# Another written-out order for a fused attention and token/channel mixer kernel: new seeds of the planner and a new order of loads

## The chip, the cores and the metric

The kernel runs on one core of one Trainium2 chip. The metric is the time of one execution on the device, in microseconds (us); lower is better. The core has five engines that run side by side and wait for each other through semaphores: TensorE (PE, matmuls; PEld is its loading of weights), VectorE (DVE), ScalarE (ACT), GpSimd (POOL), which here issues most loads, and SyncE (SP), which here issues transposing DMAs and stores. Each engine works through its own instructions strictly in the order in which they were written.

## The reference

Attention with 8 heads over 576 positions, 8 batches, a causal window of 128 and a linear bias per head, then an MLP mixer, first over the tokens and then over the channels:

```python
scores = scale * np.matmul(q, k.transpose(0, 1, 3, 2))        # q, k, v: (8, 8, 576, 64)
mask = (rel >= 0) & (rel < 128)                               # rel = pos[:, None] - pos[None, :]
scores = np.where(mask, scores + bias[None], -1e9)            # bias = -slope[h] * |rel|
attn = softmax(scores)                                        # over the last axis
x = (attn @ v), heads side by side                            # (8, 576, 512)

h = np.maximum(x.transpose(0, 2, 1) @ w_tok1, 0.0) @ w_tok2   # w_tok1 (576, 256), w_tok2 (256, 576)
u = x + h.transpose(0, 2, 1)
out = u + np.maximum(u @ w_ch1, 0.0) @ w_ch2                  # w_ch1 (512, 1536), w_ch2 (1536, 512)
```

Inputs and output are float32; the kernel computes in bfloat16 with float32 sums.

## The kernel before, in words

**Tiles.** The 576 positions of a batch are four blocks of 128 and a rest of 64. Batches go in pairs: blocks 0 to 3 belong to the first batch of a pair, 4 to 7 to the second, and block 8, the tail, holds both rests.

**Stages.** `side(b)` makes what the channel mixer of batch `b` needs. For each block the q and k tiles (`qk`) are turned (`qkT`; on PE at L681 with a copy at L687 for the first blocks, by a DMA that SP issues at L670 for the later ones), the scores are made on PE (L724), exponentiated on ACT (L759, L746), masked on DVE (L769, L751), multiplied with `v` on PE (L804) and divided by the sum of the row into `xb` (L817 and L820 on DVE, or L826 on ACT). `token_mix(b)` follows: W1 times `xb` (L849, and L859 for the tail), a relu (L867 on ACT or L868 on DVE) into `r10` or `r11`, W2 times that (L891, L887 for the tail), and the sum with `xb` into `ub` or `utl` (L909 on DVE). `ub` is turned into `uT`, on PE (L926) for the first two batches and by a DMA from SP (L917) for the others. `main(b)` is the channel mixer: chunks of WC1 times `uT` (L1087, L1072 for the first pieces of batch 0, L1131 for tails; L1008 where a unit of seven smaller products takes the place of four chunks), their relus (L1093, L1094 and others), sums on DVE (L1112 `s`, `r`), and the second product (L1328, L1220 for tails) as seven products of halves, whose weights include four sums of quarters of WC2, `WT`, made once on DVE at L598. Each product is taken up by DVE at L1291 into a buffer that is stored.

**What sets the order.** No engine's order is written by hand. Every piece of work is entered in a `Plan` with an engine, an expected cost, a rank and the buffers it uses. `Plan.run` goes through time by the plan's own costs, picks for each engine among the ready pieces by time and rank, and gives out buffers and PSUM banks; the pieces are then emitted in the order so found. That order is what the program keeps: on the chip, nothing is picked again. `side(b+1)` and `main(b)` are ranked so that they interleave. A table `SEEDS` shifts the rank of every piece in a group (stage times 10 plus a running part of 30 pieces) by a pseudo-random amount of at most `SHIFT` = 1500; groups that are not in the table are not shifted. Where a piece may run on ACT or on DVE, the plan picks that too.

**Loads.** POOL issues all loads in the order of the string `LOADS` and then block by block for the later pairs. `q2` is the q tile of block 2 of the first pair, `W1` and `W2` the two token weights (W1 brings half of `W1p` with it, `P1` brings the other half), `T0` the part `W2t` of W2 for the tail, `A0` to `A3` the quarters of WC1 and `B0` to `B3` those of WC2. A load is issued only when its buffer is free and when the load eight places earlier has landed.

**Fillers.** Early in the program, where the plan has PE waiting, `emit` puts matmuls on zeros (L1420) into a free PSUM bank. L515 zeroes a part of one `pe` buffer that a later matmul reads.

Of the kernel before, what the change touches and what calls it, by code (L numbers as in the profile page):

```python
# [64 lines left out]
def offset(o):  # L65
    seed = SEEDS.get(o.group, 0)
    z, full = (seed << 20) + o.part * 1000 + o.at, (1 << 64) - 1
    z = (z + 0x9E3779B97F4A7C15) & full
    z = ((z ^ (z >> 30)) * 0xBF58476D1CE4E5B9) & full
    z = ((z ^ (z >> 27)) * 0x94D049BB133111EB) & full  # L70
    return ((z ^ (z >> 31)) >> 11) * 2.0**-52 - 1.0 if seed else 0.0


class Plan:
# [235 lines left out]
    def emit(self, spin):  # L310
# [11 lines left out]
        for _, _, go in sorted(work, key=lambda w: w[:2]):  # L322
# [20 lines left out]
RANKH = 0  # L343
RELU = 350
SUMS_AT = 60e3
SEEDS = {4: 101440, 5: 787032, 6: 757153, 8: 103423, 10: 747690, 11: 468454, 12: 753267, 20: 739044, 21: 923522, 22: 509005, 23: 528472, 30: 196195, 31: 885075, 40: 886354, 41: 184683, 42: 921347, 50: 122991, 51: 204193, 60: 609045, 62: 920468, 70: 169615, 73: 856563, 80: 485548, 81: 308774, 82: 443378, 90: 121380, 91: 900109, 92: 158454, 100: 446306, 101: 820311, 102: 110347, 110: 183021, 111: 737037, 112: 44421, 120: 445134, 121: 47942, 122: 813192, 130: 923735, 131: 191992, 132: 371665, 140: 693539, 141: 260420, 142: 463672, 150: 60451, 151: 574542, 152: 386295, 153: 745919, 154: 632491}
GROUP = 30
SHIFT = 1500.0
UNIT_LATE = False
# [28 lines left out]
EARLY = 1  # L378


LOADS = ("q2 T0 k2 k8 k1 q1 v2 v3 q8 v1 v0 k5 v8 W2 W1 q4 q5 "
         "k4 q7 q6 k6 A2 A0 k7 v7 B0 A3 v4 A1 v5 B1 B2 B3 P1 v6")


@with_exitstack
def kernel(
# [16 lines left out]
    P = nc.NUM_PARTITIONS  # L403
# [6 lines left out]
    R = S - NC * P  # L410
# [18 lines left out]
    plan = Plan()  # L429
# [38 lines left out]
    W1 = const.tile([P, NC, DTOK], BF16, name="W1")  # L468
    W1p = const.tile([P, 2, DTOK], BF16, name="W1p")
    W2 = const.tile([P, NJ, NC * P], BF16, name="W2")  # L470
# [20 lines left out]
    pe_, act_, dve_ = nc.tensor, nc.scalar, nc.vector  # L491
# [19 lines left out]
            act_.activation(out=masks[:, e, i, :, :], in_=dist[:, :, :], func=ACT.Exp, scale=-float(slopes[h]))  # L511
    for t in plan.rings["v"].slots:
        dve_.memset(t[:, :, D : D + 1], 1.0)
    for t in plan.rings["pe"].slots[0:1]:
        dve_.memset(t[:, :, :, :, R:P], 0.0)  # L515

    held = {}
    def turns_of(pr):
# [41 lines left out]
    plan.items = []  # L560
    for item in LOADS.split():
        what, n = item[:-1], int(item[-1])
# [893 lines left out]
```

## Time and profile before

| | us |
|---|---|
| median of 3 runs | 275.4 (275.15 to 275.79) |
| the profiled execution's own time | 275.81 |
| its span, first to last instruction | 273.7 |
| PE busy | 264.7 (97%) |
| DVE busy | 230.1 (84%) |
| ACT busy | 147.6 (54%) |

The span is what the profile shows of the execution; 2.1 us of its time lie outside it. The granted TensorE clock is 1.0 over the whole span. A busy PE is counted up to the modelled end of each matmul, and those overlap: waits of PE are read from the rows that name what ended an idle time, and from the distance between starts. In rows of the timeline the columns are the start and the length in us from the span's start, the engine, the line, the operation, output and inputs, the shape, the count, and in brackets the idle time ahead of it with what ended it. In rows of the chain they are the start, the length and what it was. A `q` behind an engine's name (POOLq, SPq) marks a DMA that it issues; the length there is that of the issue.

### The profile page before, as it was taken

To read this page: it belongs to the slowest core of one execution; us is meant where nothing else is said; L and a number is where in the kernel's file an instruction comes from. 1 tells how busy PE (TensorE), PEld (TensorE's weight loads), DVE (VectorE), ACT (ScalarE), POOL (GpSimd) and SP (SyncE) were. 2 spreads that over 40 slices of the span, in tenths; PEclk is the share of its full clock that TensorE was granted. 3 is DMA by queue.
4 is the path that set the end of the run, shared out by engine and by line. 5 is a ranking of instruction groups with operands and counts; after the bars stand their busy time and mean duration, and the time that the engine had idled before them with its cause. 6 is when DMAs were issued, how large, how long until landed. Compare 5 with 4: busy or idle time off the path is not lost.

```text
span 273.7 us, 7090 instructions
## 1 busy us (share of the span) xinstructions
PE 264.7 (97%) x2803; PEld 188.5 (69%) x2832; DVE 230.1 (84%) x545; ACT 147.6 (54%) x257; POOL 113.2 (41%) x142
## 2 busy tenths in 40 slices
PE   8999999799999999999999999999999999999994
PEld 4665658475568565775778868685678676888883
DVE  7586799988996687966999889997899899957983
ACT  5492883437930694059940098428932496046820
POOL 8999646950680079303970029500920300040000
PEclk9999999999999999999999999999999999999999
DMA  8999999999999999999999959959996700540016
GB/s 156 154 172 171 192 193 179 152 168 211 129 133 148 199 157 141 163 185 193 121 155 125 237 113 113 138 114 210 188 146 98 211 2 0 79 163 14 0 41 192
DMA packets 167553, 38.71 MB, mean 141 GB/s; under 512 B 155872, under 2 KB 166496, under 8 KB 167520
## 3 DMA queue, kind: packets, MB, share of 16 engines
q0 software_dynamic: 113936, 19.51, 92.0%
q1 hardware_dynamic: 51360, 18.10, 34.6%
q10 hardware_dynamic: 2224, 0.66, 1.2%
q8 instruction: 22, 0.36, 0.6%
q14 instruction: 11, 0.09, 0.1%
HBM read 35.85 MB, written 9.44 MB: 165 GB/s over the span
## 4 chain that ended last, share of the span: by engine, by line
PE 88%; DVE 7%; DMA 2%; issue 1%; DVEq 0%; SPq 0%
PE ps L1328 22%; PE ps L1087 18%; PE ps L1008 10%; PE ps L724 6%; PE ps L804 6%; PE ps L849 5%; PE ps L891 4%; PE ps L1131 4%; PE ps L1420 3%; PE ps L1220 3%; DMA uT<-ub 2%; PE ps L681 2%; DVE WT L598 1%; PE ps L859 1%; DVE ub L909 1%
## 5 line engine op out<-in xcount | busy, mean ns | idle before, releaser
L537 POOL DMA_DIRECT2D v<-in_v_dram x40 | 34.2, 862 | 88.8 <-PE ps L804 83.1
L759 ACT ACTIVATE pe<-ps 128x1024 bf16<-128x1024 f32 (+1 forms) x62 | 56.0, 957 | 18.9 <-PE ps L724 18.5
L1087 PE MATMUL ps<-uT,WC 128*128 128x512 bf16 x214 | 55.2, 379 | 1.5 <-DMA uT<-ub 0.4
L1093 ACT ACTIVATE r<-ps 128x512 bf16<-128x512 f32 x53 | 31.1, 603 | 21.3 <-PE ps L1087 21.0
L1328 PEld LDWEIGHTS <-r 128*128 128x128 bf16 x372 | 35.6, 98 | 6.1 <-issue 0.6
L1087 PEld LDWEIGHTS <-WC 128*128 128x128 bf16 x232 | 20.6, 98 | 20.5 <-issue 0.8
L537 POOL DMA_DIRECT2D qk<-in_q_dram x38 | 32.8, 871 | 1.3 <-DMA v<-in_v_dram 1.0
L537 POOL DMA_DIRECT2D qk<-in_k_dram x38 | 32.8, 870 | 0.9 <-DMA WC<-in_moe_w_ch_dram 0.9
L769 DVE TENSOR_TENSOR pe<-pe,mask 128x1024 bf16<-128x1024 bf16 (+1 forms) x50 | 32.6, 661 | 0.5 <-ACT pe L759 0.2
L1328 PEld LDWEIGHTS <-s 128*128 128x128 bf16 x288 | 27.8, 98 | 4.0 <-issue 0.2
L820 DVE TENSOR_TENSOR xb<-ps,rt 128x256 bf16<-128x256 f32 (+1 forms) x68 | 27.5, 417 | 0.8
L804 PEld LDWEIGHTS <-pe 128*128 128x128 bf16 (+1 forms) x560 | 22.2, 98 | 7.0 <-DVE pe L769 1.3
L804 PE MATMUL ps<-v,pe 128*128 128x65 bf16 (+1 forms) x560 | 25.9, 194 | 0.5 <-DVE pe L769 0.5
L1328 PE MATMUL ps<-WC,r 128*128 128x256 bf16 x192 | 25.1, 273 | 0.1
L1328 PE MATMUL ps<-WT,s 128*128 128x256 bf16 x192 | 24.4, 273 | 0.0
L724 PEld LDWEIGHTS <-qkT 64*128 64x128 bf16 x560 | 14.7, 94 | 11.2 <-issue 9.3
L1328 PE MATMUL ps<-WT,r 128*128 128x256 bf16 x180 | 22.1, 273 | 0.0
L909 DVE TENSOR_TENSOR ub<-ps,xb 128x512 bf16<-128x512 f32 x30 | 19.1, 683 | 1.1 <-PE ps L891 0.9
L746 ACT ACTIVATE pe<-ps 128x1024 bf16<-128x1024 f32 x7 | 7.2, 1023 | 23.1 <-PE ps L724 23.1
L724 PE MATMUL ps<-qkT 64*128 64x128 bf16 (+1 forms) x304 | 19.3, 216 | 0.0
L1291 DVE TENSOR_TENSOR raw<-ps,ub 128x512 f32<-128x512 f32 x23 | 15.7, 686 | 3.3 <-PE ps L1328 3.2
L849 PE MATMUL ps<-xb,W 128*128 128x512 bf16 x57 | 15.8, 379 | 0.4
(120 smaller groups left out, 448.7 us busy)
## 6 DMA issues: line engine op xcount, KB each, us to landing
v<-in_v_dram POOLq DMA_DIRECT2D x32, 128.0 KB, 4.9
qk<-in_q_dram POOLq DMA_DIRECT2D x30, 128.0 KB, 5.0
qk<-in_k_dram POOLq DMA_DIRECT2D x30, 128.0 KB, 5.0
WC<-in_moe_w_ch_dram POOLq DMA_DIRECT2D x8, 384.0 KB, 10.4
out_dram<-raw SPq DMA_DIRECT2D x12, 256.0 KB, 2.7
out_dram<-raw SPq DMA_DIRECT2D x16, 128.0 KB, 3.7
out_dram<-raw POOLq DMA_DIRECT2D x6, 256.0 KB, 2.6
out_dram<-ob SPq DMA_DIRECT2D x5, 256.0 KB, 2.6
```

Of the source, the lines that this page charges most:

```text
L537: nc.gpsimd.dma_start(out=to()[p0 : p0 + n, :, :], in_=rows(src, b, s0, n))
L724: pe_.matmul(wide(e)[:, i, 0 if joint else kind, a:z], lhsT=ts[kb]()[e * D : (e + 1) * D, NHP + i, :], rhs=ts[blk]()[e * D : (e + 1) * D, ...
L759: act_.activation(out=pb()[:, e, :, lo:, c0:c1_], in_=wide(e)[:, :, lo:, c0:c1_], func=ACT.Exp, scale=scale)
L769: dve_.tensor_tensor(out=o, in0=o, in1=heads(mk, es), op=ALU.mult)
L804: pe_.matmul(view()[a:z, at, i, :], lhsT=pb()[:, e, i, kind, a:z], rhs=vb()[:, h, 0 : D + 1], start=m == 0, stop=m == len(mms) - 1, skip_g ...
L820: dve_.tensor_tensor(out=x4(), in0=view()[r0:r1_, :, :, 0:D], in1=rt()[r0:r1_, 0:n, :, :].broadcast_to([r1_ - r0, n, 4, D]), op=ALU.mult)
L849: pe_.matmul(t1[j]()[:, :], lhsT=W1[:, c, j * P : (j + 1) * P], rhs=xb()[:, blk, :], start=c == 0, stop=False)
L909: plan.op("DVE", 690, lambda blk=blk, u=u_of(pr, blk)[1], ht=ht, hs=hs: dve_.tensor_tensor(out=u(), in0=ht()[:, hs], in1=xb()[:, blk, :], ...
L1008: pe_.matmul(bk()[:, c * HS : (c + 1) * HS], lhsT=l(c, cb), rhs=r(cb), start=new and c == 0 and cb == 0, stop=cb == 1, skip_group_check=True)
L1087: pe_.matmul(ct()[:, :], lhsT=WC1[:, cb, t * P : (t + 1) * P], rhs=uT()[:, cb, :], start=cb == 0, stop=cb == NCB - 1)
L1093: plan.op("ACT", 600, lambda t=t, ct=ct: act_.activation(out=r2()[:, t, :], in_=ct()[:, :], func=ACT.Relu), rk, part=(r2, t), uses=[ct], o ...
L1328: pe_.matmul(of(bk, c), lhsT=l(t, c), rhs=w(t), start=first, stop=g == 1 and t == HK - 1, skip_group_check=True)
```

## The change

Two tables of the planner are replaced, and one memset goes. `SEEDS` loses some groups, gains others and has other numbers in all of them; `LOADS` names the same 35 loads in another order. The costs, rules and buffers of the planner stay, and so do all operations; which of the two engines takes a piece that either may take is found anew.

```diff
-SEEDS = {4: 101440, 5: 787032, 6: 757153, 8: 103423, 10: 747690, 11: 468454, ...
+SEEDS = {0: 517497, 4: 785877, 5: 700536, 6: 16714, 7: 413526, 8: 685397, ...
...
-LOADS = ("q2 T0 k2 k8 k1 q1 v2 v3 q8 v1 v0 k5 v8 W2 W1 q4 q5 "
-         "k4 q7 q6 k6 A2 A0 k7 v7 B0 A3 v4 A1 v5 B1 B2 B3 P1 v6")
+LOADS = ("k2 k8 q2 k1 q1 v3 v0 v1 v8 q8 v2 q7 W1 q5 q6 k6 k7 "
+         "W2 v7 v6 k5 A1 q4 A0 k4 B0 A2 v4 A3 B3 B2 v5 P1 T0 B1")
...
-    for t in plan.rings["pe"].slots[0:1]:
-        dve_.memset(t[:, :, :, :, R:P], 0.0)
```

Counted over the whole program, PE has 2839 matmuls where it had 2832; the seven more are fillers (51 where there were 44). DVE has one instruction less than before (the memset, L515) and one piece of work goes over from it to ACT. Lines behind L515 stand two lines lower in the changed kernel (L818 there is L820 here).

The first place is the end of the loads on POOL, where the weights of the channel mixer come (WC_122 is WC1, WC_123 is WC2, the rest are tiles and small weights of the token mixer). Before:

```order
L537 DMA v_75<-in_v_dram 128x8x64
L541 DMA WC_123<-in_moe_w_ch_dram 128x3x512
L541 DMA WC_122<-in_moe_w_ch_dram 128x4x384
L537 DMA v_72<-in_v_dram 128x8x64
L541 DMA WC_122<-in_moe_w_ch_dram 128x4x384
L537 DMA v_74<-in_v_dram 128x8x64
L541 DMA WC_123<-in_moe_w_ch_dram 128x3x512 x3
L541 DMA W1p<-in_moe_w_tok_dram 64x256
L537 DMA v_73<-in_v_dram 128x8x64
```

The same place on POOL in the changed kernel:

```order
L539 DMA WC_123<-in_moe_w_ch_dram 128x3x512
L539 DMA WC_122<-in_moe_w_ch_dram 128x4x384
L535 DMA v_76<-in_v_dram 128x8x64
L539 DMA WC_122<-in_moe_w_ch_dram 128x4x384
L539 DMA WC_123<-in_moe_w_ch_dram 128x3x512 x2
L535 DMA v_72<-in_v_dram 128x8x64
L539 DMA W1p<-in_moe_w_tok_dram 64x256
L539 DMA W2t<-in_moe_w_tok_dram 128x2x64
L539 DMA WC_123<-in_moe_w_ch_dram 128x3x512
```

Before, the last of the 35 loads was the v tile of block 6 (v_73); now it is the quarter B1 of WC2, and the v tiles of blocks 6 and 7 stand further up, behind W2.

The second place is DVE in the middle of `main(0)`, where it makes the sums WT and, between them, divides the values of the last blocks of batch 1 into `xb`. Before:

```order
L598 TENSOR_TENSOR WT<-WC_123 128x768
L844 COPY xt_96<-xb_92 64x512
L598 TENSOR_TENSOR WT<-WC_123,WT 128x768 x2
L817 RECIPROCAL rt_88<-ps 128x4
L1112 TENSOR_TENSOR r_103<-r_103 128x3x256
L817 RECIPROCAL rt_89<-ps 128x4
L817 RECIPROCAL rt_91<-ps 128x4
L817 RECIPROCAL rt_90<-ps 128x4
L820 TENSOR_TENSOR xb_92<-ps,rt_89 128x4x64
L820 TENSOR_TENSOR xb_92<-ps,rt_91 128x4x64
L820 TENSOR_TENSOR xb_92<-ps,rt_90 128x4x64
L598 TENSOR_TENSOR WT<-WC_123,WT 128x768
```

DVE at the same place in the changed kernel:

```order
L596 TENSOR_TENSOR WT<-WC_123 128x768
L815 RECIPROCAL rt_89<-ps 128x4
L818 TENSOR_TENSOR xb_92<-ps,rt_88 128x4x64
L818 TENSOR_TENSOR xb_92<-ps,rt_89 128x4x64
L815 RECIPROCAL rt_90<-ps 128x4
L815 RECIPROCAL rt_91<-ps 128x4
L596 TENSOR_TENSOR WT<-WC_123,WT 128x768
L818 TENSOR_TENSOR xb_92<-ps,rt_91 128x4x64
L596 TENSOR_TENSOR WT<-WC_123 128x768 x2
L596 TENSOR_TENSOR WT<-WC_123,WT 128x768
L1110 TENSOR_TENSOR s_113<-r_103,s_113 128x768
L596 TENSOR_TENSOR WT<-WC_123,WT 128x768
```

Three sums WT and the copy `xt` stood ahead of the last three divisions; now these divisions stand ahead of the four sums that need the last quarters of WC2.

The third place is DVE at the end of `token_mix(6)`, where the four sums `ub` are made that SP then turns into the `uT` of `main(6)`. Before:

```order
L1032 TENSOR_TENSOR r_103<-ps,ob_111 128x2x256
L1032 TENSOR_TENSOR r_103<-ps,ob_110 128x2x256
L1034 TENSOR_SCALAR r_103<-r_103 128x2x256 x2
L1032 TENSOR_TENSOR r_103<-ps,raw_107 128x2x256
L1034 TENSOR_SCALAR r_103<-r_103 128x2x256
L909 TENSOR_TENSOR ub_94<-ps,xb_92 128x512 x4
```

DVE at the same place in the changed kernel:

```order
L1030 TENSOR_TENSOR r_103<-ps,raw_107 128x2x256
L1032 TENSOR_SCALAR r_103<-r_103 128x2x256
L866 TENSOR_SCALAR r_98<-ps 128x512
L1030 TENSOR_TENSOR r_103<-ps,ob_110 128x2x256
L1030 TENSOR_TENSOR r_103<-ps,raw_108 128x2x256
L907 TENSOR_TENSOR ub_94<-ps,xb_92 128x512 x4
```

Two of the relus behind the joins (L1034) left DVE's row, and a relu of the token mixer (L866, which is L868 before) came into it; on PE the last product of the second stage of batch 5 (12 matmuls of 256 columns) now stands ahead of the first chunk of `main(6)` and not behind it.

More of the change, by code (lines that the diff above doesn't have):

```diff
@@ L345 @@
 SUMS_AT = 60e3
-SEEDS = {4: 101440, 5: 787032, 6: 757153, 8: 103423, 10: 747690, 11: 468454, 12: 753267, 20: 739044, 21: 923522, 22: 509005, 23: 528472, 30: 196195, 31: 885075, 40: 886354, 41: 184683, 42: 921347, 50: 122991, 51: 204193, 60: 609045, 62: 920468, 70: 169615, 73: 856563, 80: 485548, 81: 308774, 82: 443378, 90: 121380, 91: 900109, 92: 158454, 100: 446306, 101: 820311, 102: 110347, 110: 183021, 111: 737037, 112: 44421, 120: 445134, 121: 47942, 122: 813192, 130: 923735, 131: 191992, 132: 371665, 140: 693539, 141: 260420, 142: 463672, 150: 60451, 151: 574542, 152: 386295, 153: 745919, 154: 632491}
+SEEDS = {0: 517497, 4: 785877, 5: 700536, 6: 16714, 7: 413526, 8: 685397, 10: 382165, 11: 797072, 20: 274424, 21: 252221, 22: 938434, 23: 229954, 30: 618980, 31: 73962, 40: 48116, 41: 463500, 42: 138947, 50: 698411, 60: 77721, 61: 670382, 62: 980070, 70: 272112, 71: 329646, 73: 863296, 80: 860821, 81: 812390, 82: 698755, 90: 642555, 91: 36162, 92: 820492, 100: 378208, 101: 12283, 102: 666882, 110: 374839, 111: 457165, 112: 228977, 122: 958618, 130: 444343, 131: 112543, 132: 417601, 140: 895813, 141: 108506, 142: 904489, 151: 79725, 152: 698131, 153: 848768, 154: 58892}
 GROUP = 30
```

## The prediction

> **What bounds the kernel now.** I read the busy shares first, then the six stretches between the places where PE stood, then PE's waits.
>
> ```profile
> PE 264.7 (97%) x2803; PEld 188.5 (69%) x2832; DVE 230.1 (84%) x545; ACT 147.6 (54%) x257; POOL 113.2 (41%) x142
> ...
> 0.00:21.15 21.15, 19.62 (x244) 12.17 (x245) 15.33 (x54) 13.37 (x27) 19.74 (x29) 1.00 1.77 161
> 21.15:28.68 7.53, 7.32 (x69) 4.28 (x69) 5.11 (x12) 3.00 (x5) 7.38 (x10) 1.00 1.93 176
> 28.68:48.10 19.42, 19.26 (x249) 13.27 (x252) 17.76 (x45) 12.98 (x20) 10.69 (x13) 1.00 1.69 186
> 48.10:59.69 11.59, 10.13 (x87) 6.83 (x87) 10.49 (x24) 4.79 (x10) 10.31 (x14) 1.00 2.23 173
> 59.69:268.50 208.81, 206.88 (x2142) 150.70 (x2164) 179.65 (x403) 113.44 (x196) 65.04 (x78) 1.00 1.14 131
> 268.50:273.73 5.23, 1.53 (x20) 1.27 (x18) 1.74 (x11) 0.00 (x0) 0.00 (x0) 1.00 0.56 191
> ```
>
> In the stretches the columns are from and to, the length, the busy time of PE, PEld, DVE, ACT and POOL with the counts, the granted clock, the DMA share and GB/s. PE sets the pace at a full clock: from 59.69 to 268.50 us it is idle for 208.81 − 206.88 = 1.93 us. The products are the same before and after, so the change can only move PE's waits, and these are few:
>
> ```profile
> PE ps L681 <- DVE xb L820: 1.4, 1, 1.4
> PE ps L1420 <- DVE zero L499: 1.0, 1, 1.0
> PE ps L804 <- DVE pe L769: 0.5, 1, 0.5
> PE ps L1087 <- DMA uT<-ub: 0.4, 1, 0.4
> ```
>
> The columns are who waits for what, the sum, how often, and the longest. The wait of L1420 is the program's start, that of L804 lies among the fillers; both stay. The other two can go. The forecast is therefore a sum of small terms: what these two waits give, and what a new order of loads and of PE's row costs elsewhere.
>
> **Term 1: the wait at 48 us.** The chain (start, length, what), then PE's row and the last of the loads:
>
> ```profile
> 46.14 0.56 DVE WT L598
> 46.71 0.68 DVE xt L844
> 47.40 1.03 DVE WT L598 x2
> ...
> 49.32 0.33 DVE xb L820
> ...
> 49.66 0.61 PE ps L681 x8
> ```
>
> ```profile
> 47.44 0.82 PE L1328 MATMUL ps<-WC,r 128*128 128x256 bf16 x6
> 49.66 0.61 PE L681 MATMUL ps<-ident,qk 128*128 128x128 bf16 x8 [1.41 <-DVE xb L820]
> 50.10 1.89 PE L849 MATMUL ps<-xb,W 128*128 128x512 bf16 x7
> ```
>
> ```profile
> 36.93 0.91 POOL L537 DMA_DIRECT2D v<-in_v_dram  x1 [2.13 <-PE ps L724]
> ...
> v<-in_v_dram POOLq DMA_DIRECT2D x1, 128.0 KB, 9.4
> ```
>
> Six products of 256 columns at .11 from start to start end PE's work at 47.44 + .66 = 48.10; L681 starts at 49.66, so PE loses 1.56 us. It needs the PSUM bank whose values DVE divides last, and DVE had three sums WT and the copy xt in its row ahead of that (46.14 to 48.43). These values came late because the v tile of block 6 was the last load: 36.93 + 9.4 = 46.3. In the changed order v6 is the twentieth name and not the last, so its values are made long before, and DVE's divisions stand ahead of the four late sums. Stepping through DVE's row with the lengths above puts the last division at 47.0 to 47.3. PE reaches the first L849 at 47.7, counted so: the stretch from the first L1087 to the wait is 19.42 us; six L1328 (.66) now stand behind it and .22 of columns ahead of it, which leaves 18.5, from a start at 29.2 (term 2). So no wait is left, **−1.56**. The spare is .4 to .7 us; the term keeps between 0 and all of 1.56.
>
> **Term 2: the head.** The first product of the channel mixer waits for a quarter of WC1.
>
> ```profile
> 2.40 0.72 POOL L541 DMA_DIRECT2D W2t<-in_moe_w_tok_dram  x1
> 18.61 0.89 POOL L537 DMA_DIRECT2D qk<-in_k_dram  x1
> 22.09 1.53 POOL L541 DMA_DIRECT2D WC<-in_moe_w_ch_dram  x2
> ```
>
> ```profile
> W<-in_moe_w_tok_dram POOLq DMA_DIRECT2D x2, 256.0 KB, 5.4
> WC<-in_moe_w_ch_dram POOLq DMA_DIRECT2D x2, 384.0 KB, 6.9
> ```
>
> ```profile
> 24.42 1.03 PE L891 MATMUL ps<-r,W 128*128 128x512 bf16 x4
> ...
> 28.68 1.02 PE L1087 MATMUL ps<-uT,WC 128*128 128x512 bf16 x3 [0.16 <-DVE uT L930]
> ```
>
> POOL issues back to back. In both orders 25 issues stand ahead of the first quarter; W2t (.72) is replaced by a tile of .89, so the quarter is issued at 22.3 and lands, at 6.3 to 6.9, between 28.6 and 29.2. W2 was early and is now the 22nd issue, where the row has 18.61: at 18.8 + 5.4 it lands at 24.2, while L891 started at 24.42. So the first L1087 comes at about 29.2, .5 later, with .2 of other columns done ahead of it: **+0.3**. Its bounds: −.5 if the seven more fillers only fill what PE idled in this stretch and a little of the one ahead (7.53 − 7.32 and 21.15 − 19.62); +1.2 if they no longer lie in a wait: the 51 stand for 9.1 us of columns against 7.9 for the 44. I cost them at nothing, since the wait for W2 and the quarter covers them.
>
> **Term 3: the last load.** B1 takes v6's place. All loads together carry the same bytes, so the queue empties when it did, at 46.3; its issue waits for A2, eight places earlier, issued at about 26.4 by POOL's lengths and landing after the median of these loads:
>
> ```profile
> DMA to landing us min/median/max: 6.3/10.4/13.5
> ```
>
> That is 36.8, near the 36.93 of before, and gives again 46.2 to 46.3. The first product with B1 stands 17.2 us of columns behind the first L1087, at 46.4; the sums WT with it follow on DVE. **+0.1**. Ends: nothing when it lands sooner (−0), and 3.7 at the longest landing (36.8 + 13.5 = 50.3, against 46.4, less .2 of fill).
>
> The Trainium skill, "DMA: Bandwidth & Descriptors", section "Anatomy of one DMA — SWDGE (gpsimd) path", fits the time of such a DMA by 2.0 us and its bytes over 436,000 per us, which is 2.9 us for 384 KB (an estimate from that page). By it B1 would land near 40 and the first quarter near 25, terms 2 and 3 would be nought, and the sum would be .4 lower. This trace doesn't bear that out: its median is 10.4.
>
> **Term 4: the start of main(6).**
>
> ```profile
> 208.59 4.34 DMA uT<-ub
> ```
>
> ```profile
> 211.87 0.82 PE L1328 MATMUL ps<-WC,s 128*128 128x256 bf16 x6
> 213.06 1.02 PE L1087 MATMUL ps<-uT,WC 128*128 128x512 bf16 x3 [0.37 <-DMA uT<-ub]
> 213.92 1.47 PE L1328 MATMUL ps<-WT,r 128*128 128x256 bf16 x12
> ```
>
> PE is through with the six at 212.53 and starts at 213.06, .53 lost. In the changed order the twelve L1328 that follow the first chunk (1.31 us) stand ahead of it, and cover the transposing DMA. The relu that DVE took from ACT there adds some .6 to DVE's row ahead of the sums, two others leave it. **−0.5**, at worst 0.
>
> **Term 5: the start of main(3).** Here the cover shrinks.
>
> ```profile
> 109.12 0.62 PE L887 MATMUL ps<-r,W2t 128*64 128x512 bf16 x4
> ...
> 121.27 1.03 PE L1087 MATMUL ps<-uT,WC 128*128 128x512 bf16 x3
> ```
>
> ```profile
> 112.61 3.82 SPq L917 DMA_TRANSPOSE uT<-ub  x3
> ```
>
> SP ends its issues for that batch at 116.4; with some 3 us of landing the tiles are there at 119.4, 1.9 ahead of 121.27. In the changed order PE has 10.0 us of columns between the last u source and that L1087 instead of 11.7, so the spare shrinks to .2, and the tail's sum now stands behind a relu on DVE. **+0.2**, between 0 and +.8.
>
> **Term 6: all other places.** By the same count the starts of main(2), (4), (5) and (7) keep 1.1 us or more, the rows are nearly alike from 215 us on, and switches between small and large products stay at 74. But hundreds of pieces change places, and each late one costs PE some tenths that no count shows. The rows bound that: 0.9% idle in the long stretch (1.93 of 208.81), 2.8% in the second (.21 of 7.53). At 0.9% nothing changes; at 2.8% it is 5.8, or +3.9. The nearest row is the long stretch itself, and a run of before has had all its waits counted while new ones can only be found on the chip, so I take **+0.4** (−.2 to +3.9).
>
> The memset:
>
> ```profile
> 3.87 0.48 DVE L515 MEMSET pe<- 128x512 uint32 x1
> ```
>
> PE stands there in fillers and waits for loads of q and k, so its going gives 0 (at most −.3).
>
> **Sum.** −1.56 + .3 + .1 − .5 + .2 + .4 = −1.06. The profiled execution took 275.81 (span 273.73), .4 above the median of 275.4; so 274.75 in its terms, and **274.3** against the median. A difference under 0.2% (.55 us) can't be told from none; faster means under 274.85, slower over 275.95.
>
> **Rivals.**
> 1. *B1 comes too late (slower).* As the last of eight loads in flight it may land later than v6 did. PE waits at the first product with B1, and DVE, whose row keeps the order, waits at the sums WT with s sums and evicts queued behind. Landed at 47.6 the wait is 1.2, and the gain is gone but for the last tenths (275.4); from 48.2 on it is slower than before by over 0.2%; at 50.3 it gives 274.3 + 3.7 = 278.0. For it: the landings of 6.3 to 13.5. Against it: the queue's bytes are the same.
> 2. *No net change.* The spare in term 1 is under .7 us. If W2 and the first quarter come .5 to 1 later, everything behind moves, DVE's divisions included, and the 1.56 is paid in the head: about 275.4.
> 3. *New waits in the long stretch (slower).* At an idle share between that of the long stretch and 2.8% the sixth term is 2 to 3.9 instead of .4: 276 to 278. For it: DVE is 84% busy and works in a fixed row. Against it: PE's banks and the spare at main's starts have been counted and are over 1 us save at main(3).
>
> **How the numbers follow.** The forecast (273.0 to 274.85) has .50; rival 2 .20; rival 1 .12; rival 3 .18. So faster .50, same .20, slower .30. Below 273.0 lies about .04 (all terms at their lower ends), above 277.4 about .14 (rivals 1 and 3 at their upper ends). The range 273.0 to 277.4 holds the rest.
>
> **What would show it.** Right: no wait of PE for DVE's division near 48 us and an L849 at 47.5 to 48.5; first L1087 at 28.9 to 29.5; last load landing by 46.5; no row "L1087 waits for uT" near 212; a wait under .8 near 119. Wrong: a wait of PE or of DVE's WT for WC in 46 to 51 us (rival 1); the first L1087 after 30 (rival 2); an idle share of PE over 1.5% between 60 and 268 us (rival 3).

## The result, and the profile after

| | before | changed |
|---|---|---|
| median of 20 runs, us | 275.47 (274.91 to 276.10) | 274.08 (273.75 to 275.18) |
| ratio to before | | 0.9956, 95% interval 0.9945 to 0.9967 |
| the profiled execution's own time, span | 275.81, 273.7 | 275.12, 273.4 |

The change makes the kernel 1.4 us faster by the medians (1.2 by the ratio on record, which is not the quotient of the medians). The forecast was 274.3. The profiled execution of the changed kernel is among the slowest of its 20 runs, 1.0 over the median, so a second profile of the same kernel (time 274.06, span 272.3; a_again below) stands beside it from here on. In the changed kernel lines behind L515 stand two lower than before.

The stretches of the changed kernel, cut at the same places of the program as those of before (columns as there):

```profile
21.24:29.87 8.63, 8.34 (x96) 5.08 (x95) 6.85 (x17) 3.65 (x8) 7.84 (x11) 1.00 1.85 179
29.87:48.53 18.66, 18.66 (x240) 12.61 (x238) 16.66 (x45) 15.19 (x30) 10.62 (x14) 1.00 1.64 189
48.53:59.82 11.29, 11.29 (x102) 7.42 (x99) 10.65 (x21) 4.25 (x8) 8.69 (x12) 1.00 2.11 152
59.82:268.40 208.58, 207.66 (x2160) 150.71 (x2157) 180.63 (x404) 112.88 (x192) 65.92 (x80) 1.00 1.16 132
```

PE's waits in the first profile, then in the second:

```profile
PE ps L1418 <- DVE zero L499: 1.0, 1, 1.0
PE ps L1129 <- DMA uTt<-utl: 0.9, 1, 0.9
PE ps L924 <- DVE ub L907: 0.3, 1, 0.3
```

```profile
PE ps L1418 <- DVE zero L499: 1.0, 1, 1.0
PE ps L924 <- DVE ub L907: 0.3, 1, 0.3
```

Both waits that the forecast counted on are gone: PE is busy from 29.87 to 59.82 us without a gap, and no L1085 (L1087 before) waits for `uT`. In their place stands one of .92 us for the turned tail of `main(3)`, which the second profile does not have. PE's row at the two early places, and the last load:

```profile
28.73 0.40 PE L924 MATMUL ps<-ident,ub 128*128 128x128 bf16 x4 [0.29 <-DVE ub L907]
...
29.87 1.46 PE L1085 MATMUL ps<-uT,WC 128*128 128x512 bf16 x6
...
48.53 1.89 PE L847 MATMUL ps<-xb,W 128*128 128x512 bf16 x8
```

```profile
37.00 0.74 POOL L539 DMA_DIRECT2D WC<-in_moe_w_ch_dram  x1 [1.23 <-DMA WC<-in_moe_w_ch_dram]
...
WC<-in_moe_w_ch_dram POOLq DMA_DIRECT2D x1, 384.0 KB, 9.5
```

The last load lands at 37.00 + 9.5 = 46.5 and nobody waits for it.

Since two orders are compared, starts alone mislead: work stands ahead of a place in one and behind it in the other. The table below shows *lost time* instead: the start of an instruction less the column time of all matmuls ahead of it in PE's row (each form's usual distance from start to start; fillers count as lost). A difference between two columns is what PE lost on the way. A switch between products of 64 rows or columns (the scores, L722, for one) and full ones loses some .1 and is in it too: six products end at 212.16 + .66 = 212.82 in the changed kernel, and the scores behind them start at 212.91. Some traces lack 28 or 29 records of matmuls (before has 2803, for 2832 weight loads); those are counted as done. The names of the experiments are explained below; "before" to "b_m6" share the old order up to 46 us, the others the new one.

| profile | first L849 | first L1087 | L849 of batch 1 | main(1) | main(2) | main(3) | main(5) | last matmul |
|---|---|---|---|---|---|---|---|---|
| before | 13.68 | 14.39 | 16.82 | 16.94 | 18.34 | 19.70 | 21.74 | 24.50 |
| b_norms | 13.80 | 14.99 | 15.91 | 17.49 | 18.88 | 20.24 | 22.32 | 24.54 |
| b_late | 15.08 | 15.79 | 16.69 | 17.72 | 19.11 | 20.47 | 22.56 | 24.78 |
| b_m6 | 14.18 | 14.88 | 16.92 | 17.03 | 18.44 | 19.80 | 21.89 | 24.39 |
| changed | 14.24 | 15.36 | 16.37 | 16.85 | 18.00 | 20.46 | 22.50 | 24.44 |
| a_again | 14.00 | 15.12 | 16.13 | 16.61 | 17.76 | 19.37 | 21.41 | 23.35 |
| a_v7late | 14.43 | 15.53 | 16.54 | 17.02 | 18.16 | 19.59 | 21.64 | 23.58 |
| a_sums | 13.96 | 15.99 | 17.00 | 17.88 | 19.02 | 20.66 | 22.71 | 24.65 |

From the last matmul's start to the end of the span it is 3.9 us before and 3.7 after.

### The profile page after: what moved, and what is told of

It reads as the page before. It is cut to its first block, busy times and chain, and to the rows that moved or that the text cites. A ratio compares the mean times of both kernels' runs of the same rounds, so it can differ in the third digit from the quotient of the medians.

```text
span 273.4 us, 7106 instructions
## 1 busy us (share of the span) xinstructions
PE 267.6 (98%) x2839; PEld 190.0 (69%) x2839; DVE 230.4 (84%) x543; ACT 148.9 (54%) x258; POOL 112.9 (41%) x142
## 4 chain that ended last, share of the span: by engine, by line
PE 94%; DMA 3%; DVE 1%; issue 0%; DVEq 0%
PE ps L1326 25%; PE ps L1085 19%; PE ps L1006 10%; PE ps L802 7%; PE ps L722 7%; PE ps L847 5%; PE ps L889 4%; PE ps L1418 4%; PE ps L1129 4%; PE ps L1218 3%; DMA uTt<-utl 3%; PE ps L679 2%; PE ps L857 1%; PE ps L885 1%; PE ps L1070 1%; PE ps L924 1%
## 5 line engine op out<-in xcount | busy, mean ns | idle before, releaser
L1085 PE MATMUL ps<-uT,WC 128*128 128x512 bf16 x232 | 55.4, 380 | 0.0
L1091 ACT ACTIVATE r<-ps 128x512 bf16<-128x512 f32 x51 | 29.9, 599 | 18.4 <-PE ps L1085 18.1
L1085 PEld LDWEIGHTS <-WC 128*128 128x128 bf16 x232 | 21.1, 97 | 20.8
L818 DVE TENSOR_TENSOR xb<-ps,rt 128x256 bf16<-128x256 f32 (+1 forms) x68 | 27.3, 416 | 0.7
L1326 PE MATMUL ps<-WC,r 128*128 128x256 bf16 x192 | 24.4, 273 | 0.0
L722 PEld LDWEIGHTS <-qkT 64*128 64x128 bf16 x560 | 14.8, 94 | 10.5 <-issue 8.5
L722 PE MATMUL ps<-qkT 64*128 64x128 bf16 (+1 forms) x304 | 19.3, 216 | 0.1
L815 DVE RECIPROCAL rt<-ps 128x4 f32<-128x4 f32 (+1 forms) x76 | 12.6, 176 | 6.0 <-PE ps L802 5.1
L847 PE MATMUL ps<-xb,W 128*128 128x512 bf16 x64 | 16.4, 379 | 0.0
```

Of the source, the lines that this page charges most:

```text
L722: pe_.matmul(wide(e)[:, i, 0 if joint else kind, a:z], lhsT=ts[kb]()[e * D : (e + 1) * D, NHP + i, :], rhs=ts[blk]()[e * D : (e + 1) * D, ...
L818: dve_.tensor_tensor(out=x4(), in0=view()[r0:r1_, :, :, 0:D], in1=rt()[r0:r1_, 0:n, :, :].broadcast_to([r1_ - r0, n, 4, D]), op=ALU.mult)
L847: pe_.matmul(t1[j]()[:, :], lhsT=W1[:, c, j * P : (j + 1) * P], rhs=xb()[:, blk, :], start=c == 0, stop=False)
L1085: pe_.matmul(ct()[:, :], lhsT=WC1[:, cb, t * P : (t + 1) * P], rhs=uT()[:, cb, :], start=cb == 0, stop=cb == NCB - 1)
L1091: plan.op("ACT", 600, lambda t=t, ct=ct: act_.activation(out=r2()[:, t, :], in_=ct()[:, :], func=ACT.Relu), rk, part=(r2, t), uses=[ct], o ...
L1326: pe_.matmul(of(bk, c), lhsT=l(t, c), rhs=w(t), start=first, stop=g == 1 and t == HK - 1, skip_group_check=True)
```

## The experiments

Each is timed against the kernel before on the same chip in the same session (its medians there: 275.36, 275.47 and 275.91). In the names, `a` starts from the changed kernel and `b` from the kernel before. The moves use one hook where the program is put out; each pair in `MOVES` puts one piece of work, by its number in the plan, ahead of another, and nothing else changes:

```diff
-        for _, _, go in sorted(work, key=lambda w: w[:2]):
+        work.sort(key=lambda w: w[:2])
+        for n, m in MOVES:
+            at = [w[1] for w in work]
+            one = work.pop(at.index(n))
+            work.insert([w[1] for w in work].index(m), one)
+        for _, _, go in work:
```

In these kernels all lines of the program stand six lower than in the one they start from.

### The wait at 48 us

**b_norms**, divisions first:

```diff
+MOVES = [(375, 144), (140, 144), (142, 144)]
```

> The kernel before with one move in DVE's row: the copy xt and two sums WT that stand ahead of the last divisions of batch 1 now stand behind them; the loads are as they were, v6 last. Theory (order in DVE's row): values of blocks 6 and 7 are ready at 46.9 to 47.6, the divisions end at 48.1 to 48.4, PE's wait of 1.56 at 48 us goes; what DVE does later gives part of it back, so -0.8 to -1.5, to 274.0 to 274.7. Rival (v6's late landing at 46.35 sets it): the divisions cannot begin earlier, -0.3 to 0.

Measured: 275.94, ratio 1.0014 (0.9998 to 1.0030). PE's longest wait, PE's row and DVE's row:

```profile
PE ps L1334 <- DVE raw L1297: 1.4, 1, 1.4
```

```profile
48.75 0.61 PE L687 MATMUL ps<-ident,qk 128*128 128x128 bf16 x8
...
52.81 1.47 PE L1334 MATMUL ps<-WT,s 128*128 128x256 bf16 x12 [1.40 <-DVE raw L1297]
```

```profile
50.06 1.62 DVE L604 TENSOR_TENSOR WT<-WC,WT 128x768 bf16<-128x768 bf16 x3
51.60 0.55 DVE L1118 TENSOR_TENSOR s<-s,r 128x768 bf16<-128x768 bf16 x1
52.07 0.68 DVE L1297 TENSOR_TENSOR raw<-ps,ub 128x512 f32<-128x512 f32 x1
```

In time both expectations fail. The wait at 48 us goes whole, so v6's landing does not force it. But 1.40 us come back 4 us later: the divided tiles are early, and the first evict (`raw`), whose PSUM bank PE needs for its next product, now stands behind the displaced sums. DVE is full from 44 to 55 us; this order of its row moves the wait and does not remove it.

**b_late**, and the sums that nobody needs yet go down too:

```diff
+MOVES = [(375, 144), (142, 144), (288, 297), (287, 297), (140, 308), (144, 308)]
```

> The kernel before with one move more than in the run that put the divisions first: xt and the sum WT that is needed first stand behind the divisions, and two other sums WT (used by PE only from 61 us on) and two sums of r and s (used from 57 us on) go down to the places just ahead of their use. The loads and PE's row stay. Theory (between 44 and 55 us DVE is full, and works on sums that nobody needs for 6 to 14 us; with these out of the way the whole wait goes): no wait of PE over .3 between 46 and 56 us, -1.0 to -1.6, to 273.8 to 274.4. Rival (the loads are needed too, since v6 lands at 46.35): a wait of 1 us or more of PE for DVE appears somewhere between 46 and 56 us, 275.0 or more.

Measured: 275.01, ratio 0.9984 (0.9971 to 0.9996). Two of PE's waits:

```profile
PE ps L855 <- DMA W<-in_moe_w_tok_dram: 0.9, 1, 0.9
...
PE ps L1334 <- DVE raw L1297: 0.5, 1, 0.5
```

A gain of .46, half of the smallest that the theory gave; the rival's time, without its wait of 1 us. The wait for the evict shrinks from 1.40 to .52, so the sums were part of it. With v6 last, neither of the two orders of DVE's row that were tried keeps the 1.56: the values of blocks 6 and 7 can't be divided before v6 is there, and then xt, the divisions and the evict come in a bunch. (In this profile W1 landed late, which moves the whole head by about 1 us and by itself shortens the wait at 48 us.)

**a_sums**, the reverse on the changed kernel:

```diff
+MOVES = [(141, 340), (143, 340)]
```

> The changed kernel with two of the late sums WT (those that need the last loaded quarter) put ahead of the last divisions in DVE's row, much as the kernel before has it. Theory (the order in DVE's row sets the wait at 48 us): the divisions end 1.0 to 1.1 us later, PE's first L847 of batch 1 waits for them by about as much, and the time is +0.9 to +1.1 (about 275.1). Rival (the place of v6 among the loads sets it, and DVE's order is second): no wait over .3, within +0.3.

Measured: 274.72, ratio 0.9963 (0.9948 to 0.9977); the changed kernel in the same session 274.49. Two waits:

```profile
PE ps L895 <- DMA W<-in_moe_w_tok_dram: 0.7, 1, 0.7
...
PE ps L853 <- ACT xb L830: 0.4, 1, 0.4
```

(ACT's division waits for the reciprocals that DVE makes behind the sums.) From the first L1087 to main(1) PE loses 17.88 − 15.99 = 1.9 here against 1.49 in both profiles of the changed kernel. That .4 is less than half of what was expected, between theory and rival. The late W2 of this execution (first row) put PE .5 to .9 behind, which gives DVE that much spare; the time difference of .23 is inside the spread of both.

**loads_only** and **seeds_only**, one table of the change alone:

```diff
-LOADS = ("q2 T0 k2 k8 k1 q1 v2 v3 q8 v1 v0 k5 v8 W2 W1 q4 q5 "
+LOADS = ("k2 k8 q2 k1 q1 v3 v0 v1 v8 q8 v2 q7 W1 q5 q6 k6 k7 "
...
```

> The kernel before with the new LOADS and the old SEEDS; the planner finds the order of all engines anew. Theory (v6 at the end of the loads is what made DVE late): v6 lands before 30 us, no wait of PE over .5 for DVE between 44 and 56 us, 274.2 to 275.0. Rival (the two tables fit each other; old seeds with new loads give an order with waits of its own): one or more new waits of PE over .7, 275.5 or more.

> The kernel before with the new SEEDS and the old LOADS. Theory: v6 lands at about 46.3, the divisions of blocks 6 and 7 come after that, and PE waits 1 us or more for DVE between 46 and 56 us; only the gains at main(6) and in main(7) can remain, 274.9 to 275.6. Rival (the order of DVE's row is found anew and covers it): 274.5 or less.

Measured: loads_only 278.41, ratio 1.0091 (1.0077 to 1.0105); seeds_only 275.63, ratio 0.9996 (0.9985 to 1.0008). The stretches and waits of loads_only:

```profile
30.00:56.00 26.00, 25.86 (x290) 16.21 (x289) 23.30 (x58) 15.77 (x27) 18.57 (x24) 1.00 1.82 177
56.00:100.00 44.00, 40.58 (x428) 26.73 (x426) 34.59 (x82) 20.80 (x31) 12.43 (x15) 1.00 1.54 152
```

```profile
PE ps L724 <- DMA qkT<-qk: 1.7, 1, 1.7
PE ps L804 <- DVE pe L769: 1.2, 1, 1.2
```

With v6 early the place at 48 us is clean (.14 idle in 26 us), as the theory said, and the rival holds as well: 3.4 us are lost in the next 44 us to waits that neither kernel has. With the new seeds alone the time is that of before, though PE is idle for only .56 us between 30 and 56 us and no wait is over .4, where the theory wanted 1 us at one place; where it loses the rest was not followed. The two tables only work as a pair. (seeds_only also has the memset of the kernel before; leaving it out was not tried alone.)

### The start of main(6)

```diff
+MOVES = [(1088, 1178), (1089, 1178)]
```

> The kernel before with one move in PE's row: the twelve L1328 behind the first chunk of main(6) stand ahead of it, as in the changed kernel. Theory after reading the trace (their PSUM bank comes free with the evict that ends at 212.77, so they can't start before 212.8): PE waits .25 instead of .53, -0.2 to -0.3, to about 275.2. Rival (the prediction's term): the wait goes whole, -0.5, to about 274.9.

Measured: 275.72, ratio 0.9991 (0.9978 to 1.0003), which separates neither. PE's row does:

```profile
212.02 0.82 PE L1334 MATMUL ps<-WC,s 128*128 128x256 bf16 x6
212.97 1.47 PE L1334 MATMUL ps<-WT,r 128*128 128x256 bf16 x12
214.27 1.03 PE L1093 MATMUL ps<-uT,WC 128*128 128x512 bf16 x4
```

The six end at 212.02 + .66 = 212.68 and the twelve start at 212.97: .29 is lost to the evict, and the chunk behind them doesn't wait. In the changed kernel eight score products (L722) stand in that gap as well, and nothing is lost. The profiles show another thing: how long the last `uT` takes. First row b_m6, second b_norms, which have the same order there:

```profile
uT<-ub SPq DMA_TRANSPOSE x1, 4.7
```

```profile
uT<-ub SPq DMA_TRANSPOSE x2, 2.4
```

Where it takes 2.4, as in b_norms and b_late, the old order doesn't wait at main(6) either. So the wait of .53 before was one that comes and goes: two of these four profiles have it.

### The tail of main(3)

**a_again**, the changed kernel unaltered.

> The changed kernel once more, unaltered, for a second profile and its spread. Theory (a collision that comes and goes): the profiled execution of 275.12 us is 1.04 over the median of 274.08 because PE waited .92 us at 118.7 for the transposing DMA uTt, which in most executions does not happen; a profile of an execution near 273.8 then shows no such wait, or one under .2, and times fall into two clusters about 1 us apart. Rival (the wait is always there): the profile shows .8 to 1.1 at that place whatever its time, and the spread of the times comes from elsewhere.

Measured: 274.49 (273.83 to 274.85, 6 runs), ratio 0.9948 (0.9931 to 0.9965). The theory holds for the wait: a profile of 274.06 doesn't have it. These six times don't fall into two clusters; they lie evenly over 1 us. Of the 20 of the result 12 lie under 274.25 and 7 over 274.6, so two groups are not excluded; but a_head below has the wait again (.4) in an execution of 274.11, and a_v7late, whose profile has no wait, has times over 274.6 too, so the wait alone does not make them. Loads and transposes issued between 111.5 and 112.9 us, in the first profile, in the second, and in a_v7late (us to landing at the end of each row), and PE's wait in the first:

```profile
qk<-in_k_dram POOLq DMA_DIRECT2D x2, 64.0 KB, 5.9
uTt<-utl SPq DMA_TRANSPOSE x1, 6.8
```

```profile
qk<-in_k_dram POOLq DMA_DIRECT2D x2, 64.0 KB, 5.1
uTt<-utl SPq DMA_TRANSPOSE x1, 5.0
```

```profile
qk<-in_k_dram POOLq DMA_DIRECT2D x1, 64.0 KB, 4.0
uTt<-utl SPq DMA_TRANSPOSE x1, 3.7
```

```profile
118.69 1.03 PE L1129 MATMUL ps<-uTt,WC 128*128 128x256 bf16 x8 [0.92 <-DMA uTt<-utl]
```

SP issues the transpose at 111.7 to 111.9 in all three. It takes 6.8, 5.0 or 3.7 us, as it shares the DMA engines with the end of a burst of loads that POOL issued up to 112.9. PE needs it at 117.6 to 117.8: with 6.8 it waits, with 5.0 it doesn't. In the first profile it lands together with the last load of the burst (118.65 and 118.71), in the second 1.6 us ahead of it (116.64 and 118.23). The other runs bear the burst out as the cause: 6.0 to 6.4 in a_b3, a_sums and a_head, which keep the loads, and 3.7 and 3.2 in a_best and a_steady, which have the v tile late. The Trainium skill, "DMA: Bandwidth & Descriptors", section "Issuing engines are not separate DMA queues", says that DMAs of all issuing engines run on the same 16 DMA engines and interleave; these rows agree.

**a_b3** covers the wait with products:

```diff
+MOVES = [(600, 700), (601, 700)]
```

> The changed kernel with one move in PE's row: the twelve L1326 that follow the first tail group of main(3) (L1129) now stand ahead of it, which puts 1.31 us of work over the wait for uTt. Theory (collision that comes and goes): the cluster of times at 274.6 to 275.2 goes, the median falls by .1 to .4 to about 273.8, and the lowest times stay. Rival (always there): every time falls by .9 to 1.0, to about 273.1. Second rival (the wait moves to the first chunk of main(3), which needs the last uT some 1.7 us later): nothing changes, 274.1.

Measured: 275.18, ratio 0.9990 (0.9977 to 1.0004), .7 slower than the changed kernel in the same session, against all three expectations. PE's waits say why:

```profile
PE ps L1332 <- DVE raw L1295: 0.5, 1, 0.5
PE ps L1135 <- ACT r2t L1140: 0.4, 1, 0.4
```

The twelve products need a PSUM bank that DVE's evict frees only then, and the two tail groups, now close together, need the relu between them. A wait that comes and goes was traded for two that seem to be always there: the lowest of the 12 times is 274.89, against 273.83 for the changed kernel.

**a_v7late** takes bytes out of the burst:

```diff
+MOVES = [(89, 96)]
```

> The changed kernel with one move in POOL's row: the v tile of block 7 of the third pair, used only after 160 us, is loaded after the v tiles of block 8 (issued at 128 us) and not ahead of the four last q and k loads of the burst that ends at 112.9 us. Theory (the transposing DMA of the tail, issued at 111.8, lands at 116.6 or at 118.7 as it comes to lie ahead of or behind the last of these loads): the burst ends .9 us sooner, uTt lands by 116.8 in the profile, PE's wait at 118 us doesn't occur, the times over 274.6 go, median 273.8 to 273.9, the lowest stay at 273.7. Rival (the spread has other causes): the times spread as before, 273.8 to 275.2, median 274.1 to 274.5.

Measured: 274.48 (273.97 to 275.00, 6 runs), ratio 0.9967 (0.9955 to 0.9979). The transpose behaves as the theory said (3.7 us, no wait). The median does not fall, and the times spread as before: the rival is right on the spread.

### The head, and all together

```diff
+MOVES = [(240, 246)]
```

> The changed kernel with one move in DVE's row: the sum ub of block 2 of batch 0 stands ahead of the copy uT of block 1 (both were released at the same time). Theory (the head is set by the chain ub, transpose, copy uT, first L1085, and not by the landing of WC1): PE's wait of .3 for ub goes, the first L1085 comes .3 earlier relative to the first L889, time -0.2 to -0.35. Rival (DVE's row up to its first evict at 51.8 sets the next stage anyway, spare .1): L1085 comes earlier, but PE waits for the evict by as much at 52 us, 0.

Measured: 274.26 (273.75 to 274.79, 6 runs), ratio 0.9960 (0.9949 to 0.9972). Between the first L849 and the first L1087 PE loses 14.87 − 13.83 = 1.04 in this profile against 1.12, 1.12 and 1.10 in the three of the changed head (changed, a_again, a_v7late): under .1 is gained where the theory gave .3, as one of .2 for the copy `uT` comes in place of the wait for `ub`. The time is .2 below the unaltered kernel of an earlier session, which is inside the spread. The profile shows no wait for the evict at 52 us, so the rival does not hold either.

**a_best** adds the late v tile and moves four sums of DVE down:

```diff
+MOVES = [(89, 96), (240, 246), (271, 396), (143, 297), (140, 300), (144, 300)]
```

> The changed kernel with both moves above (the late v tile, and ub ahead of the copy) and four sums of DVE between 47 and 51 us (three WT, one of r) moved down to just ahead of their use at 56 to 61 us. Theory: the three add up, -0.5 to -0.8 against the changed kernel, 273.3 to 273.6, with times within .6 of each other. Rival: DVE's spare is not needed, and only the moves of the head and the load count: 273.5 to 273.8.

**a_steady** loads W2 earlier instead of moving the sums:

```diff
+MOVES = [(89, 96), (240, 246), (27, 25), (332, 345), (333, 346)]
```

> The changed kernel with three things that differ from execution to execution taken off PE's path: the late v tile and ub ahead of the copy, as in the runs before, and W2 loaded three places earlier (ahead of k6 and k7), with the turns of block 6 ahead of those of block 7 on PE and DVE to fit. Theory (what spreads the times is the landing of W2, 24.6 to 25.6 against 24.8 at which the relus are done, and of uTt): no wait of PE for W2 or uTt, times within .6 of each other, 273.5 to 273.9. Rival (the spread comes from the first loads of q, k and W1 ahead of 21 us): as wide as before, 273.8 to 274.8.

Measured: a_best 274.31 (273.99 to 274.62, 5 runs), ratio 0.9960 (0.9948 to 0.9972); a_steady 274.29 (273.94 to 274.71, 5 runs), ratio 0.9937 (0.9924 to 0.9950). Neither reaches the times that the theories gave (the rival of a_steady, a spread that comes from the loads ahead of 21 us, gave 273.8 to 274.8), and none of the four versions can be told from the changed kernel, whose interval is 0.9945 to 0.9967. In a_steady a new wait shows, at 157 us. a_v7late and a_best have the same late v tile and no such wait, so its cause stays open:

```profile
PE ps L728 <- DMA qkT<-qk: 0.4, 1, 0.4
```

## Why the prediction was right, and where it was not

The time came out .2 below the forecast and within its range, on the side that was given .50. Its sum was −1.06 and the measured difference −1.39 (the interval of the ratio: −.9 to −1.5). None of its signs of being wrong showed in the two profiles of the changed kernel. Of its signs of being right the two lost waits and the last load came true; the first L1087 at 29.87 and 29.62 lies behind its 29.5, the L849 at 48.53 and 48.29 is at the end of its window (47.5 to 48.5), and the .92 near 119 is over its .8 in one profile of two. By terms, from the lost times:

**Term 1 (the wait at 48 us, −1.56): the mechanism was right, the size somewhat less.** From the first L1087 to the L849 of batch 1 PE loses 1.01 after the change, and 2.43 and 2.04 before (the second in b_m6, whose head was .5 later; v6 is last in either, so a later head shortens the wait). That is −1.0 to −1.4. The forecast took the wait of one execution as an amount, and took all of it as kept. To main(1) PE loses another .48 after and .11 before, so there the two orders stand nearly equal (16.94 and 17.03 before; 16.85, 16.61 and 17.02 after); but that isn't the wait coming back. The first profile has no gap there, and .2 of the difference are two switches, since eight score products stand ahead of main(1) after the change and behind it before. Counted to main(2) the two orders have the same number of switches: PE loses 2.6 there from the first L1087 on after, and 3.95 and 3.56 before. So .9 to 1.3 is kept, .25 less than the wait of the same trace. What b_norms shows for the old loads, a DVE so full that the wait comes back, does not happen with the new ones: PE has no gap from 29.87 to 59.82 us.

**Term 2 (the head, +0.3): right in sign, +0.4.** From the first L849 to the first L1087 PE loses 1.10 to 1.12 in three profiles with the new head (1.4 in a_b3 and 2.0 in a_sums, which wait for W2), and .70 to .71 in three with the old one (1.19 in b_norms, which waits .4 for a q tile). At the first L1087 the four profiles with the old head stand between 14.39 and 15.79, median 14.94; five with the new one, a_b3 with 15.45 among them, between 15.12 and 15.99, median 15.45. The forecast named W2 and the quarter of WC1. W2 came .5 later than reckoned, since its 5.4 became

```profile
W<-in_moe_w_tok_dram POOLq DMA_DIRECT2D x1, 256.0 KB, 5.9
```

in both profiles of the changed kernel and 6.8 in a_sums. In a_sums PE waited for it, .7. In the first profile of the changed kernel it landed at 24.74, while PE was busy with the turns ahead of its first product, and cost nothing:

```profile
24.10 1.07 PE L679 MATMUL ps<-ident,qk 128*128 128x128 bf16 x16
25.00 0.60 PE L889 MATMUL ps<-r,W 128*128 128x512 bf16 x2
```

What set the head there was the chain of `ub`, transpose and copy, which led to the L1085 at 29.87; its quarter of WC1, which landed at 29.22, was not the last to come. The profile of before happened to have the earliest head of all four, which hid that this place differs by 1.4 us between executions of one order.

**Term 3 (B1 last, +0.1): right.** It landed at 46.5 (forecast 46.2 to 46.3) and PE did not wait. Rival 1 did not occur.

**Term 4 (main(6), −0.5): the place was right, and half of the amount.** The wait exists in some executions only. From main(5) to the last matmul PE loses 1.94 in all four profiles with the new order, and 2.76, 2.50, 2.22 and 2.22 before; the .28 between 2.22 and 1.94 belongs to term 6.

**Term 5 (main(3), +0.2): the place was right, the cause was another.** The forecast thought of the four `uT`; it was the tail `uTt`, whose time depends on a burst of loads. From main(2) to main(3) PE loses 1.36 in all four profiles with the old order, and with the new 1.43, 1.61 and 1.64 without the wait and 2.46 with it: +.1 to +.3, or +1.1 in a bad execution, which the given end of +.8 did not reach.

**Term 6 (all other places, +0.4): wrong in sign.** From main(6) to the last matmul it is −.28 (.95 before, .67 after). PE's row at 247 us, before and after, shows where: the second group starts .67 behind the first before, and .44 after.

```profile
247.03 0.60 PE L1008 MATMUL ps<-uT,WC 128*128 128x256 bf16 x4
247.70 0.60 PE L1008 MATMUL ps<-tt,WC 128*128 128x256 bf16 x4
```

```profile
247.22 0.60 PE L1006 MATMUL ps<-uT,WC 128*128 128x256 bf16 x4
247.66 0.60 PE L1006 MATMUL ps<-tt,WC 128*128 128x256 bf16 x4
```

Another −.2 lies behind the last matmul: the last two stores take 2.1 us to land before and 1.7 to 1.8 after. Perhaps the store ahead of them is in their way: DVE's last full evict stands behind ten small memsets of `zero` before and starts at 269.21, behind five after and starts at 268.61. This was not tried. Together about −.5. The step that failed took the idle share of the long stretch as something that a new order can only equal or raise. The share itself was misread: of the 1.93 us, .37 is the wait for `uT`, and nearly all of the rest are holes that missing matmul records leave, most of them .05 each. b_m6 has all its records and the same order up to main(6), and its PE is idle for .18 of the 212 us from 56 to 268.

Put together: at main(2) the new order is .2 to .7 ahead (18.34 and 18.44 before; 18.00, 17.76 and, in a_v7late, 18.16 after), which is term 1 less the head and less what differs ahead of the first L849. With −.28 and −.2 of term 6, 0 to −.5 of term 4 and +.1 to +.3 of term 5 the pieces come to −.4 to −1.6, around the measured −1.39 but too wide to check it. That the forecast was so near is in part luck: term 1 gave .3 to .7 less than forecast, term 6 some .9 more, and the two errors cancel.

What stays open: what makes the landing of W1 and W2 differ by up to 1.4 us between executions, and with it most of the spread; and what the extra 2 us of single transposes collide with at 209 us, where POOL loads nothing.

## What to carry to other kernels

A wait that can be named in a trace is worth its length only if the engine that is waited for has time to spare behind it (b_norms: 1.56 us gone, 1.40 back 4 us later); look at how full that engine is for the next few microseconds, and which of its later results PE needs. A trace can lack records: compare the matmuls with the weight loads before an idle share is read as waiting. One profile shows one execution: take a second before a wait or a landing is made a term of a sum, and count waits for DMAs as a chance, not as an amount. In a written order, a move that covers a wait needs the bank and the inputs of what covers it to be ready at that time.

## What was not expected of the hardware

The same transposing DMA, issued at the same time of the same program, took 5.0 us in one execution and 6.8 in another, and 3.2 to 3.7 in three kernels with 128 KB of loads less in flight ahead of it. Elsewhere single transposes took 4.3 to 4.7 us where the same ones took 2.3 to 2.4 in another execution, with no load in flight. The weight tile of 256 KB that the first products of the token mixer wait for landed between 21.1 and 22.5 us in four executions of the same loads (19.8 to 21.1 for the one ahead of it).
